# A four-layer attention kernel: the normalisation's reciprocal root as Ln and Exp on ScalarE, and new limits for the planner

## Chip, core and metric

The kernel runs on one core of a Trainium2 chip. The metric is the device time of one execution in microseconds. A core has TensorE (PE, the matrix multiplier, with a separate stream of weight loads), VectorE (DVE), ScalarE (ACT), GpSimd (POOL) and SyncE (SP, which issues DMAs). Each works through its own list of instructions in order and waits on semaphores that the others raise.

## What is computed

One sequence of 2048 tokens with 512 features goes through four layers, A, B, A, B. Each layer adds to its input the result of an attention over the normalised input, with 32 heads of 16 features.

```
x = x + A(layernorm(x));  x = x + B(layernorm(x));  (both once more)

layernorm: (x - mean) / sqrt(var + 1e-5)     # no scale, no shift

A: 4 segments of 512 tokens; per segment and head
   a_dot = softmax(q k^T / 4 + causal mask) v
   a_mem = phi(q) M / (phi(q) z + 1e-6)      # phi(t) = t + 1 if t > 0 else exp(t)
   o = g * a_mem + (1 - g) * a_dot           # g = sigmoid(beta)
   M += phi(k)^T v;  z += sum phi(k)
B: softmax(q k^T / 4) v over all 2048 tokens
both: then o @ wo
```

## The kernel before, in words

The Python program is a planner. It plays the whole work through with estimated durations, and writes five lists of instructions in the order in which its model would start them (`Sched.estimate`, L133; for DVE and POOL `Sched.queue`, L164, and `Sched.resolve`, L180, which models that the two hold each other up at a shared port). The chip gets the lists.

**Units.** The scores are computed transposed, in banks: one PSUM bank holds the scores of 128 keys and 512 queries of one head. A B layer has 32 heads x 4 query segments x 16 key blocks = 2048 such banks. An A layer keeps the causal ten of sixteen 128 x 128 blocks, packed into 2.5 banks for each head and segment: 32 x 4 x 2.5 = 320 banks. Together that is 2 x 2048 + 2 x 320 = 4736. The main loop (`attention`, L2192) goes by units. A unit (`unit`, L1831) takes three banks from the front of the groups that are ready, or two where other banks go to DVE in the same unit: PE writes the scores (K and masked Q, named KB or KA and qm), and **one ACT instruction at L1912 takes the exp of the two or three banks** into pT. PE multiplies pT by V in a later unit; a column of ones in V gives the softmax's denominator.

**Banks on DVE.** DVE takes other banks away from ACT. `dx_first` (L1373) writes at L1381 an integer whose bits, read as bfloat16, are a coarse exp of the score; two further copies with a constant added to the bits are made by POOL (`pool_copy`, L1454, at L1462) or DVE (L1437, and L1480 for two pairs at once). PE multiplies all three by V and adds them up, so that such a bank goes through PE three times and not once. The buffers for it are dxt and, once they are idle, the space of KA, QA, VA, wA and wB; in the profile the groups at L1381 and L1462 carry these names. Which bank may be taken is decided in `dx_pick` (L1301). There TAKEN caps the share of a B group's banks, and TAKEN_A the number of banks of an A group.

**Background.** Projections, normalisation, phi, memory update and output projection are generators (`task_A`, `task_B` and others) that yield what they need and what they cost in PE and DVE time. `background` (L1614) and `bg_one` (L1559) run one step after another between the units, as far as credits allow. A need ("at", n) holds a step back until unit step n, and a need ("free", ...) (in `met`, L1533) until the model has the named buffers ready shortly after ACT's current end; both are used by phi (L962), whose Exp on ACT (L966) is followed two steps later by two DVE instructions (L969, L971).

**Normalisation** (`ln_part`, L856) works on four tiles of 128 tokens at a time, 16 times in all. For each tile DVE computes mean and variance (L864, L866). Then the reciprocal root for the four, on 128 x 4 numbers: at the first normalisation by Sqrt on ACT (L872), a small Exp that brings the table of Exp back (L873), and a reciprocal on DVE (L875). At the other 15 DVE does it alone: add epsilon (L877), a first guess by integer arithmetic on the bits (L879), and two Newton rounds of three instructions (L882, L883, L884), with a yield ahead of each round. `normalize` (L887) applies mean and root to a tile at L893, on DVE, or on POOL where POOL_XN is set; the tile then goes through a transposing DMA (`ln_tiles`, L924). The first normalisation uses `ln_first` (L899) and PE's transposes (L722).

**Limits.** PLAN (from L413) holds 76 rows of limits. `set_limits` (L2187) installs row k when the unit number reaches 20k. The limits say among other things how many banks DVE may take (TAKEN, TAKEN_A), when POOL takes copies or other work (POOL_C, POOL_D, POOL_XN, POOL_PHI, POOL_QM), how late an engine may be for a step to be issued (DVE_LATE, DX_LATE, EARLY, HURRY), and how the background is sorted (ORD).

PE also multiplies by a tile of zeros where its modelled activity falls below a limit (`keep_busy`, L655, and `fill_gap`, L679, issued at L675 and L702). Most matmuls carry line L675 (the helper `mm`), and evacuations of projections L749 (ACT) or L751 (DVE).

Of the kernel before, what the change touches and what calls it, by code (L numbers as in the profile page):

```python
# [5 lines left out]
dt = mybir.dt  # L6
ACT = mybir.ActivationFunctionType
# [11 lines left out]
RSQRT_MAGIC = 1597463007.0  # L19
# [72 lines left out]
class Sched:  # L92
# [86 lines left out]

    def resolve(self):  # L180
# [5 lines left out]
        while i < len(D) or j < len(G):  # L186
            if i < len(D):
                r = D[i]
                x = max(pd + r[2], r[3] + r[1]) - r[1]
            if j < len(G):  # L190
                q = G[j]
                y = max(pg + q[2], q[3] + q[1]) - q[1]
            if j == len(G) or i < len(D) and x <= y:
                if r[4] and j < len(G) and q[4] and y - x < RACE:
                    x = max(x, y + q[1] - PORT)
                if r[4]:
                    for a, z in lg:
                        if a + 20 - RACE < x < z - PORT:
                            x = z - PORT
                    ld.append((x, x + r[1]))  # L200
                pd = r[5] = r[0].end = x + r[1]
                i += 1
            else:
                if q[4]:
                    for a, z in ld:
                        if a < y < z - PORT_G:
                            y = z - PORT_G
                    lg.append((y, y + q[1]))
                pg = q[5] = q[0].end = y + q[1]
                j += 1  # L210
# [199 lines left out]
class Builder:  # L410
# [3 lines left out]
        0: dict(TAKEN_A=1, FILL_DVE=400, MASK_PE=800, PE_LOW=7, GAP=3, QMIN=3, OPART=0, DIV_LATE=2500, PACE=2, DX_LATE=1700, HURRY=1500, POOL_QM=1, POOL_C=0),  # L414
        1: dict(ACT1=300, MARGIN=600, R_LATE=2200, NEAR=5, CR_W=1300, CR_B=1800, R_PAIRS=2, DIV_LATE=800, TAKEN=0.5, DVE_LATE=800, BG_BANK=100, PHI_LATE=300, OPART=3, NEARW=20, POOL_C=2000, DX_LAG=1, POOL_D=2500, REST=8, EARLY=500, POOL_QM=1, DX_FIN=3000, DMA_LATE=1200, TRADE=400, FILL_DVE=400, ORD=-7, PACE=12, DMA_STEPS=2, HOLD_AT=12, PE_B=2),
        2: dict(FILL_DVE=400, MASK_PE=800, GAP=3, BG_BANK=400, QMIN=3, LOW=20, POOL_QM=1, ACT1=600, R_PAIRS=2, PE_LOW=7, DX_LATE=1700, DX_FIN=3000, OPART=0, HOLD_AT=12, PE_A=4, NEAR_A=50, TRADE=0, TAKEN_A=1, PART=3, DMA_LATE=700, CR_B=1200, SLACK=350),
        3: dict(R_LATE=1200, NEARW=40, PAIRS=999, MASK_PE=800, LEVEL=3, TAKEN=0.5, LOW=20, MARGIN=600, TAKEN_A=1, EARLY=300, OPART=0, QUAD=0, FILL=0.47, DX_BANK=900, CR_A=1200, DX_LATE=700, CARRY_W=1500, PART=3, CR_W=2200, HOLD_MAX=0, DVE_LATE=1700, FILL_DVE=400, BUSY_WAIT=500, ACT1=300, QMIN=3, PE_LOW=7, PE_A=6, TRADE=0, DVE_LATE_LOW=2500, POOL_D=2500, PACE=7, PE_B=6, DVE_FIN=1500, ORD=3),
        4: dict(R_LATE=1200, NEARW=40, PAIRS=999, MASK_PE=800, LEVEL=3, TAKEN=0.5, LOW=20, MARGIN=600, TAKEN_A=1, EARLY=300, OPART=0, QUAD=0, FILL=0.47, DX_BANK=900, CR_A=1200, DX_LATE=700, CARRY_W=1500, PART=3, CR_W=2200, HOLD_MAX=0, DVE_LATE=1700, FILL_DVE=400, BUSY_WAIT=500, ACT1=300, QMIN=3, PE_LOW=7, PE_A=6, TRADE=0, DVE_LATE_LOW=2500, POOL_D=2500, PACE=7, PE_B=6),
        5: dict(ACT1=300, NEAR=8, TAKEN_A=1, SLACK=550, PV_SKIP=900, FILL_DVE=400, BACK=8, CR_W=1900, NEARW=40, OPART=0, TAKEN=0.4, LOW=20, DVE_LATE=800, QWAIT=8, HOLD_AT=40, PHI_LATE=0, REST=20, POOL_D=2500, R_LATE=1200, MARGIN=350, EARLY=300, QUAD=0, CR_A=1700, CARRY_W=1500, PART=3, BUSY_WAIT=500, PE_LOW=7, PE_A=6, HURRY=4000, PAIRS=999, LEVEL=3, DX_BANK=900, DX_LATE=700, QMIN=3, TRADE=0, DVE_LATE_LOW=2500, PACE=7, DVE_FIN=1500),
        6: dict(MARGIN=350, R_LATE=1200, DX_LATE=900, TAKEN_A=1, EARLY=300, CARRY_W=1500, PART=3, OPART=2, GAP=3, QUAD=0, QWAIT=8, HOLD_SEGS=2, POOL_XN=1, NEAR=8, SLACK=550, PV_SKIP=900, FILL_DVE=400, CR_W=1900, LOW=20, PHI_LATE=0, REST=12, PE_A=6, POOL_WAIT=0, FIT=3, AHEAD=1000, POOL_QM=1, DVE_LATE=800, POOL_D=2500, LEVEL=1, BACK=8, TAKEN=0.4, BUSY_WAIT=500, QMIN=3, DVE_LATE_LOW=2500, PACE=7, DVE_FIN=200),  # L420
        7: dict(R_LATE=1200, NEARW=40, PAIRS=999, MASK_PE=800, LEVEL=3, TAKEN=0.4, LOW=30, MARGIN=350, TAKEN_A=1, EARLY=300, OPART=3, QUAD=0, FILL=0.47, DX_BANK=900, CR_A=1200, DX_LATE=900, CARRY_W=1500, PART=3, CR_W=2200, HOLD_MAX=0, DVE_LATE=1700, FILL_DVE=400, BUSY_WAIT=500, ACT1=300, DMA_LATE=1200, GAP=3, QWAIT=8, NEAR=8, PE_A=6, POOL_QM=1, DVE_LATE_LOW=2500, PACE=7, DVE_FIN=200, HURRY=1500),
        8: dict(R_LATE=1200, NEARW=40, PAIRS=999, MASK_PE=800, LEVEL=3, TAKEN=0.4, LOW=30, MARGIN=500, TAKEN_A=1, EARLY=300, OPART=3, QUAD=0, FILL=0.47, DX_BANK=900, CR_A=1200, DX_LATE=900, CARRY_W=1500, PART=3, CR_W=2200, HOLD_MAX=0, DVE_LATE=1700, FILL_DVE=400, BUSY_WAIT=500, ACT1=300, DMA_LATE=1200, QWAIT=8, NEAR=8, PV_SKIP=900),
        9: dict(MARGIN=600, NEAR=3, PV_SKIP=100, FILL_DVE=100, BUSY_ROOM=900, FILL=0.4, CR_W=1500, CARRY_W=400, R_PAIRS=2, OPART=2, GAP=3, DVE_LATE=800, QMIN=1, HOLD_AT=40, POOL_QM=1, ACT1=300, DX_LATE=900, REST=8, CR_B=1800, DX_LAG=1, BACK=6, LOW=14, BUSY_WAIT=0, POOL_D=1200, PART=3, PHI_LATE=0, EVAC_ACT=800, RUSH0=40, HURRY=1500, AHEAD=1000),
        10: dict(MARGIN=600, NEAR=3, PV_SKIP=100, FILL_DVE=100, BUSY_ROOM=900, FILL=0.4, CR_W=1500, CARRY_W=400, R_PAIRS=2, OPART=4, GAP=3, DVE_LATE=800, QMIN=1, HOLD_AT=40, POOL_QM=1, ACT1=300, DX_LATE=900, REST=8, CR_B=1800, DX_LAG=1, BACK=6, LOW=14, BUSY_WAIT=500, POOL_D=1200, PART=3, PHI_LATE=0, EVAC_ACT=800, RUSH0=40, HURRY=1500, AHEAD=1000, RUSH=120),
        11: dict(R_LATE=1500, DX_LATE=700, REST=12, NEAR=8, TAKEN_A=1, R_NEAR=50, PV_SKIP=500, FILL_DVE=400, BUSY_ROOM=900, CR_W=1300, DX_LAG=1, LOW=20, HOLD_SEGS=2, BACK=6, R_PAIRS=2, BG_BANK=100, EVAC_ACT=100, EARLY=500, CR_A=1200, POOL_QM=1, POOL_D=1200, DVE_LATE=1700, POOL_C=4000, PORT_FREE=900, PART=0),
# [348 lines left out]
    def setup(self):  # L774
# [16 lines left out]
        def pool(fn, writes, reads=()):  # L791
            self.op("pool", fn, reads=reads, writes=writes)
# [94 lines left out]
    def normalize(self, s, k, i):  # L887
# [7 lines left out]
        if eng == "pool":  # L895
            self.cr_dve += 420
# [1456 lines left out]
```

## Time and profile before

| | us |
|---|---|
| median of three runs | 1659.27 |
| lowest and highest of them | 1659.11, 1660.82 |
| the profiled execution's own time | 1659.6 |
| its span, first to last instruction | 1657.9 |
| the part outside the span | 1.7 |

The granted clock of TensorE in the profiled execution was 0.998 of full speed. The profile's busy time is the time in which an engine has an instruction in work. A group's row gives line, engine, operation, written and read tiles, shape and number; then total busy time and mean ns of one; then the idle time just before, and what ended it. "L1912 <- PE" in a list of waits means that L1912 waited for PE. In a stretch's row a busy time stands for each engine with its number of instructions, then the granted clock, the share of the DMA engines and GB/s.

### The profile page before, as it was taken

The numbers are of one execution on the slowest core, as the hardware profiler recorded it, in microseconds if no ns is written. First come the engines' busy times: TensorE is split into PE (matmuls) and PEld (weight loads), VectorE is DVE, ScalarE is ACT, GpSimd is POOL, SyncE is SP. The second block draws the span as 40 slices with busy tenths as digits, with TensorE's granted clock in tenths as the row PEclk, the third lists the DMA queues.
The fourth block names the chain that finished last, engine by engine and source line by source line (L and its number), as shares of the span: only waits on it lengthen the run. The fifth ranks groups of instructions, "written<-read, shape, count | busy, mean of one in ns | idle before, by whom it ended". The sixth has DMA issues, their size and how long they took to land.

```text
span 1657.9 us, 45400 instructions
## 1 busy us (share of the span) xinstructions
PE 1567.7 (95%) x19612; PEld 565.5 (34%) x19684; DVE 1432.7 (86%) x2387; ACT 1621.5 (98%) x1552; POOL 1206.4 (73%) x1295
## 2 busy tenths in 40 slices
PE   8999999999999999999999998999999999999999
PEld 5553435222223535222235222432222222222236
DVE  5768686989999696999978998878999999999996
ACT  8899999999999999999999999999999999999998
POOL 3332223589899354799775996468999999999985
PEclk9999999999999999999999999999999999999999
DMA  6111211001120232200211101112000200000110
GB/s 185 37 24 26 40 26 29 14 2 30 30 55 14 69 71 43 56 14 11 62 24 40 40 24 39 23 19 53 2 18 20 46 12 16 21 11 11 24 14 19
DMA packets 148425, 54.47 MB, mean 33 GB/s; under 512 B 128768, under 2 KB 147712, under 8 KB 148224
## 3 DMA queue, kind: packets, MB, share of 16 engines
q1 hardware_dynamic: 148224, 51.56, 14.4%
q8 instruction: 154, 2.52, 0.6%
q14 instruction: 47, 0.39, 0.1%
HBM read 18.88 MB, written 2.10 MB: 13 GB/s over the span
## 4 chain that ended last, share of the span: by engine, by line
ACT 58%; PE 24%; DVE 14%; POOL 2%; DMA 1%; issue 1%; SPq 0%; ACTq 0%; DVEq 0%; POOLq 0%
ACT pT L1912 56%; PE ps L675 23%; DVE KA L1381 3%; DVE dxt L1381 2%; DVE wA L1381 2%; ACT amem L966 1%; DVE wB L1381 1%; DMA oT<-ob 1%; POOL dxt L1462 1%; DMA tb<-ub 0%; DVE wA L1480 0%; DVE lnst L864 0%; DVE dxt L1480 0%; DVE oT L1198 0%; DVE VA L1480 0%
## 5 line engine op out<-in xcount | busy, mean ns | idle before, releaser
L1912 ACT ACTIVATE pT<-ps 128x1024 bf16<-128x1024 f32 (+1 forms) x1506 | 1589.5, 1211 | 23.4 <-PE ps L675 20.4
L675 PE MATMUL ps<-qm,KB 32*128 32x512 bf16 x4096 | 543.3, 385 | 54.4 <-ACT pT L1912 35.9
L675 PE MATMUL ps<-pT,VB 128*17 128x512 bf16 x2744 | 475.5, 384 | 3.0 <-DVE wB L1381 1.1
L1462 POOL TENSOR_TENSOR dxt<-dxt,shift 128x512 int32<-128x512 int32 (+1 forms) x300 | 322.7, 1086 | 127.2 <-DVE dxt L1381 92.6
L1381 DVE TENSOR_SCALAR KA<-ps 128x512 uint16<-128x512 f32 (+1 forms) x414 | 322.6, 799 | 20.6 <-PE ps L675 18.4
L675 PEld LDWEIGHTS ps<-qm,KB 32*128 32x128 bf16 x4096 | 140.3, 91 | 556.0 <-ACT pT L1912 443.6
L1381 DVE TENSOR_SCALAR dxt<-ps 128x512 uint16<-128x512 f32 (+1 forms) x346 | 262.5, 774 | 26.2 <-PE ps L675 24.4
L1462 POOL TENSOR_TENSOR QA<-KA,shift 128x512 int32<-128x512 int32 (+1 forms) x192 | 211.2, 1108 | 89.3 <-DVE KA L1381 88.8
L675 PE MATMUL ps<-dxt,VB 128*17 128x512 bf16 x1140 | 243.0, 382 | 0.6 <-POOL dxt L1462 0.6
L675 PEld LDWEIGHTS ps<-pT,VB 128*17 128x17 bf16 x2744 | 110.8, 87 | 274.5 <-issue 256.2
L1462 POOL TENSOR_TENSOR VA<-KA,shift 128x512 int32<-128x512 int32 (+1 forms) x178 | 187.1, 1059 | 14.1 <-DVE QA L1437 6.4
L1926 POOL TENSOR_SCALAR_AFFINE_SELECT pT<-pT 128x256 bf16<-128x256 bf16 (+4 forms) x136 | 70.2, 530 | 174.3 <-ACT pT L1912 174.2
L1462 POOL TENSOR_TENSOR wA<-wA,shift 128x512 int32<-128x512 int32 x150 | 161.8, 1093 | 17.6 <-DVE wA L1381 15.7
L1381 DVE TENSOR_SCALAR wA<-ps 128x512 uint16<-128x512 f32 (+1 forms) x168 | 133.0, 809 | 8.7 <-PE ps L675 7.9
L675 PE MATMUL ps<-wA,VB 128*17 128x512 bf16 x624 | 138.0, 381 | 0.0
L675 PE MATMUL ps<-QA,VB 128*17 128x512 bf16 x474 | 133.5, 381 | 0.0
L1462 POOL TENSOR_TENSOR wB<-wB,shift 128x512 int32<-128x512 int32 (+1 forms) x118 | 126.2, 1083 | 6.9 <-DVE wB L1381 5.2
L675 PE MATMUL ps<-VA,VB 128*17 128x512 bf16 x474 | 130.2, 381 | 0.5 <-POOL VA L1462 0.4
L675 PE MATMUL ps<-KA,VB 128*17 128x512 bf16 x474 | 116.6, 381 | 0.0
L1381 DVE TENSOR_SCALAR wB<-ps 128x512 uint16<-128x512 f32 (+1 forms) x137 | 105.5, 785 | 7.0 <-PE ps L675 6.4
L675 PE MATMUL ps<-wB,VB 128*17 128x512 bf16 x486 | 108.2, 381 | 0.1
L675 PE MATMUL ps<-qm,KA 32*128 32x128 bf16 (+2 forms) x1536 | 93.3, 254 | 10.6 <-ACT pT L1912 7.6
(174 smaller groups left out, 2043.9 us busy)
## 6 DMA issues: line engine op xcount, KB each, us to landing
wB<-in_B_wqkv_dram SPq DMA_DIRECT2D x48, 128.0 KB, 2.4
wA<-in_A_wk_dram SPq DMA_DIRECT2D x16, 128.0 KB, 2.3
wA<-in_A_wq_dram SPq DMA_DIRECT2D x16, 128.0 KB, 2.4
wA<-in_A_wv_dram SPq DMA_DIRECT2D x16, 128.0 KB, 2.4
out_dram<-x SPq DMA_DIRECT2D x8, 256.0 KB, 2.3
x<-in_A_x_dram SPq DMA_DIRECT2D x3, 512.0 KB, 10.9
wB<-in_B_wqkv_dram SPq DMA_DIRECT2D x1, 1536.0 KB, 13.9
oT<-ob SPq DMA_TRANSPOSE x63, 2.5
```

Of the source, the lines that this page charges most:

```text
L675: self.sc.add("pe", lambda e: e.matmul(out, lhsT, rhs, start=start, stop=stop, skip_group_check=True), reads=reads, banks=[(bank, "w", all ...
L966: self.op("act", lambda e: e.activation(et, src, ACT.Exp), reads=bsrc, writes=self.b_amem, ns=1023, gap=915)
L1381: self.op("dve", lambda e: e.tensor_scalar(d, o, SCALE * LOG2E * 128, 127.0 * 128 + EXP_BIAS, op0=ALU.mult, op1=ALU.add), writes=self.b_dx ...
L1462: self.op("pool", lambda e: e.tensor_tensor(d, s, c, ALU.add), reads=src + [self.b_shift] + [first] * k, writes=dst, ns=165 + 1.75 * n, ga ...
L1912: self.sc.add("act", (lambda dst, src: lambda e: e.activation(dst, src, ACT.Exp, scale=SCALE))(dst, src), writes=self.b_pT[slot * 3 + i:sl ...
L1926: self.op("pool", (lambda blk, pat: lambda e: e.affine_select(blk, blk, pattern=pat, compare_op=ALU.is_ge, fill=0.0, base=0, channel_multi ...
```

## The change

The reciprocal root becomes exp(-0.5 ln(var + eps)), in two ACT instructions for all 16 normalisations. One instruction in the setup loads a table set that holds both functions. The Newton rounds on DVE, the Sqrt and the small Exp at the start are gone. At all but the first normalisation the Ln waits for a ("free", ...) need, and the Exp for the next unit step.

```diff
@@ setup
+        self.sc.add("act", lambda e: e.preload_act_table_set("natural_log_exp_and_others"), ns=1283, gap=1283)
         for bk in (SUMS, MISC):
@@ ln_part
         bw = self.b_lnw[k]
-        yield [], 0, 400
-        v, y, tt = w[:, k, 0, :], w[:, k, 1, :], w[:, k, 2, :]
+        v, y = w[:, k, 0, :], w[:, k, 1, :]
         var = st[:, k, :, 7]
-        if (L, s) == (0, 0):
-            self.op("act", lambda e: e.activation(v, var, ACT.Sqrt, bias=self.eps[:, 0:1]), reads=self.b_lnst[k] + [self.b_eps], writes=[bw], ns=230)
-            self.op("act", lambda e: e.activation(self.eps[:, 1:2], self.eps[:, 0:1], ACT.Exp), reads=[self.b_eps], writes=[self.b_eps], ns=1500)
+        first = (L, s) == (0, 0)
+        if not first:
+            yield [("free", [bw], self.b_lnst[k])], 0, 0
+        self.op("act", lambda e: e.activation(v, var, ACT.Ln, bias=self.eps[:, 0:1]), reads=self.b_lnst[k] + [self.b_eps], writes=[bw], ns=300, gap=215)
+        if not first:
+            yield [("at", self.step + 1)], 0, 0
+        self.op("act", lambda e: e.activation(y, v, ACT.Exp, scale=-0.5), reads=[bw], writes=[bw], ns=300, gap=215)
+        if first:
             self.parity()
-            self.op("dve", lambda e: e.reciprocal(y, v), reads=[bw], writes=[bw], ns=165)
-            return k
-        self.op("dve", lambda e: e.tensor_scalar(v, var, LN_EPS, None, op0=ALU.add), reads=self.b_lnst[k], writes=[bw], ns=165)
-        vi, yi = v.bitcast(dt.int32), y.bitcast(dt.int32)
-        self.op("dve", lambda e: e.tensor_scalar(yi, vi, -0.5, RSQRT_MAGIC, op0=ALU.mult, op1=ALU.add), reads=[bw], writes=[bw], ns=165)
-        for it in range(2):
-            yield [], 0, 560
-            self.op("dve", lambda e: e.scalar_tensor_tensor(tt, y, -0.5, y, op0=ALU.mult, op1=ALU.mult), reads=[bw], writes=[bw], ns=165)
-            self.op("dve", lambda e: e.tensor_tensor(tt, tt, v, ALU.mult), reads=[bw], writes=[bw], ns=165)
-            self.op("dve", lambda e: e.scalar_tensor_tensor(y, tt, 1.5, y, op0=ALU.add, op1=ALU.mult), reads=[bw], writes=[bw], ns=165)
         return k
```

Where POOL_XN is set, the normalised tile is made by two POOL instructions with one per-partition operand each, instead of one with two:

```diff
@@ normalize
-        eng = "pool" if self.POOL_XN else "dve"
...
+        if self.POOL_XN:
+            self.op("pool", lambda e: e.tensor_scalar(xn, self.x[:, t, :], mean, 0.0, op0=ALU.subtract, op1=ALU.add), reads=[self.b_x[t], self.b_lnst[k][i]], writes=[self.b_xn[n]], ns=762, gap=720)
+            self.op("pool", lambda e: e.tensor_scalar(xn, xn, rstd, 0.0, op0=ALU.mult, op1=ALU.add), reads=[self.b_lnw[k]], writes=[self.b_xn[n]], ns=762, gap=720)
+        else:
```

In the planner's model of DVE and POOL, an instruction's readiness is worked out again from the moved ends of the DVE and POOL instructions that it waits for:

```diff
+    def late_ready(self, r):
+        op, ready = r[0], r[3]
+        for d in op.deps:
+            if d.eng == "dve" or d.eng == "pool":
+                ready = max(ready, d.end + (SOON.get((d.eng, op.eng)) or LAG[d.eng]))
+        return ready
@@ resolve
-                x = max(pd + r[2], r[3] + r[1]) - r[1]
+                x = max(pd + r[2], self.late_ready(r) + r[1]) - r[1]
...
-                y = max(pg + q[2], q[3] + q[1]) - q[1]
+                y = max(pg + q[2], self.late_ready(q) + q[1]) - q[1]
```

In PLAN, 70 of the 76 rows change, in 1 to 43 limits each; they were chosen by playing the lists through with random delays. The changes that touch who does the work, with the values that hold without an entry in the row (0 for all three):

| limit | rows and values before > after |
|---|---|
| TAKEN_A | 1, 23, 56, 61: 0 > 1; 47: 0 > 2; 15, 69, 70: 0 > 5; 17: 1 > 0 |
| POOL_XN | 8, 24, 28, 48: 0 > 1; 61: 1 > 0 |
| POOL_PHI (1: phi's L969 on POOL) | 6, 20, 21, 26, 35, 42, 46, 73: 0 > 1 |

TAKEN (the share of a B group that DVE may take) rises in 11 rows and falls in 7; POOL_C and POOL_D (how far POOL may be behind DVE to take a copy) rise in 16 and 14 and fall in 10 and 8.

More of the change, by code (lines that the diff above doesn't have):

```diff
@@ L420 @@
-        6: dict(MARGIN=350, R_LATE=1200, DX_LATE=900, TAKEN_A=1, EARLY=300, CARRY_W=1500, PART=3, OPART=2, GAP=3, QUAD=0, QWAIT=8, HOLD_SEGS=2, POOL_XN=1, NEAR=8, SLACK=550, PV_SKIP=900, FILL_DVE=400, CR_W=1900, LOW=20, PHI_LATE=0, REST=12, PE_A=6, POOL_WAIT=0, FIT=3, AHEAD=1000, POOL_QM=1, DVE_LATE=800, POOL_D=2500, LEVEL=1, BACK=8, TAKEN=0.4, BUSY_WAIT=500, QMIN=3, DVE_LATE_LOW=2500, PACE=7, DVE_FIN=200),
+        5: dict(ACT1=300, NEAR=8, TAKEN_A=1, PV_SKIP=900, FILL_DVE=400, BACK=8, CR_W=2200, NEARW=40, OPART=0, TAKEN=0.4, LOW=20, DVE_LATE=800, QWAIT=8, HOLD_AT=40, PHI_LATE=0, REST=20, POOL_D=2500, R_LATE=1200, MARGIN=350, EARLY=300, QUAD=0, CR_A=1700, CARRY_W=1500, PART=3, BUSY_WAIT=500, PE_LOW=7, PE_A=6, HURRY=4000, PAIRS=999, LEVEL=3, DX_BANK=900, DX_LATE=700, QMIN=3, TRADE=0, DVE_LATE_LOW=2500, PACE=7, DVE_FIN=1500, MASK_PE=800, FILL=0.47),
@@ new lines @@
+        23: dict(PAIRS=999, MASK_PE=800, LEVEL=3, TAKEN=0.5, LOW=14, MARGIN=500, TAKEN_A=1, EARLY=300, OPART=0, QUAD=0, FILL=0.4, DX_BANK=900, CR_A=1200, CARRY_W=400, PART=3, CR_W=2200, HOLD_MAX=0, DVE_LATE=1700, FILL_DVE=400, BUSY_WAIT=500, ACT1=300, QMIN=3, PE_LOW=7, TRADE=0, DVE_LATE_LOW=2500, POOL_D=500, ORD=23, BG_BANK=100, EVAC_ACT=1500, PV_SKIP=100, BUSY_ROOM=300, R_PAIRS=2, POOL_QM=1, CR_B=1800, DX_LAG=1, BACK=6, AHEAD=1000, DMA_STEPS=2, PE_B=6, DMA_LATE=0),
+        24: dict(R_LATE=1200, NEARW=40, PAIRS=999, MASK_PE=800, LEVEL=3, TAKEN=0.4, LOW=30, MARGIN=500, TAKEN_A=1, EARLY=300, OPART=3, QUAD=0, FILL=0.47, DX_BANK=900, CR_A=1200, DX_LATE=900, CARRY_W=1500, PART=3, CR_W=2200, HOLD_MAX=0, DVE_LATE=1700, FILL_DVE=400, BUSY_WAIT=500, ACT1=300, DMA_LATE=1200, QWAIT=3, NEAR=8, PV_SKIP=900, SPARE=160, POOL_XN=1),
@@ new lines @@
+        47: dict(ACT1=300, MARGIN=600, R_LATE=2200, EVAC_ACT=800, NEAR=10, CR_W=1300, CR_B=1800, R_PAIRS=2, DIV_LATE=2500, TAKEN=0.5, DVE_LATE=800, BG_BANK=100, PHI_LATE=300, OPART=3, NEARW=20, POOL_C=1000, DX_LAG=1, POOL_D=2500, REST=12, EARLY=500, POOL_QM=1, DX_FIN=3000, DMA_LATE=1200, PE_LOW=7, PORT_FREE=150, TRADE=400, RATE=2, DX_LATE=700, FILL=0.53, CARRY_W=1500, LN1_AT=6, FILL_DVE=400, POOL_WAIT=0, BUSY_ROOM=300, RUSH=40, REST_A=6, TAKEN_A=2, SPARE=60),
+        48: dict(ACT1=200, DX_LATE=700, NEAR=10, PV_SKIP=200, EARLY=500, FILL=0.47, CR_B=1800, CARRY_W=1500, OPART=2, MASK_PE=200, DIV_LATE=800, DVE_LATE=800, BG_BANK=100, QUAD=0, FILL_DVE=400, R_LATE=2200, POOL_C=2000, BACK=8, POOL_D=2500, RUSH0=40, AHEAD=1000, MARGIN=600, PE_B=6, DMA_LATE=700, QMIN=4, DX_FIN=3000, SLACK=250, HURRY=4000, TRADE=0, POOL_QM=1, FIT=3, POOL_XN=1),
@@ L490 @@
+        75: dict(REST=8, SLACK=700, R_NEAR=10, R_PAIRS=2, NEARW=90, PAIRS=999, LEVEL=1, LOW=14, GAP=1, DVE_LATE=800, BG_BANK=400, QUAD=0, POOL_WAIT=300, PV_SKIP=100, BACK=6, FILL=0.47, PART=0, LN1_AT=3, EARLY=300, DIV_LATE=2500, MARGIN=350, POOL_C=1000, ACT1=300, MASK_PE=200, POOL_D=1200, BUSY_ROOM=300, CR_W=1500, TAKEN=0.5, POOL_XN=1, CR_A=1700, CR_LOW=2000, DX_BANK=700, RATE=2, QWAIT=3, DVE_FIN=1500, POOL_QM=1, DMA_LATE=0),
     }
```

140 lines of the change are left out of this document (66 added, 74 removed).

## The prediction

> **What bounds the kernel now.** I read the busy shares and the chain of the page first, then the stretches by stage, then ScalarE's waits, then the groups that the edit touches.
>
> ```profile
> span 1657.9 us, 45400 instructions
> ...
> PE 1567.7 (95%) x19612; PEld 565.5 (34%) x19684; DVE 1432.7 (86%) x2387; ACT 1621.5 (98%) x1552; POOL 1206.4 (73%) x1295
> ...
> ACT 58%; PE 24%; DVE 14%; POOL 2%; DMA 1%; issue 1%; SPq 0%; ACTq 0%; DVEq 0%; POOLq 0%
> ```
>
> ScalarE (ACT) is busy for 98% of the span and holds 58% of the chain; TensorE (PE) holds 24% of it. So a microsecond of ACT work is worth about a microsecond of time, as long as PE follows.
>
> ```profile
> 0.00:300.00 300.00, 278.03 (x4007) 137.98 (x4045) 215.88 (x479) 284.11 (x237) 95.15 (x159) 0.99 0.23 51
> 300.00:550.00 250.00, 237.98 (x2718) 72.62 (x2717) 227.23 (x357) 248.71 (x248) 219.91 (x229) 1.00 0.12 26
> 550.00:700.00 150.00, 142.09 (x1992) 62.50 (x2007) 117.81 (x248) 148.75 (x133) 74.58 (x92) 1.00 0.28 62
> 700.00:850.00 150.00, 145.47 (x1669) 41.88 (x1669) 138.82 (x219) 148.07 (x150) 134.87 (x136) 1.00 0.13 28
> 850.00:900.00 50.00, 46.00 (x758) 24.92 (x761) 39.44 (x68) 48.72 (x44) 28.99 (x37) 1.00 0.14 26
> 900.00:1050.00 150.00, 139.65 (x1554) 41.46 (x1552) 135.50 (x223) 146.93 (x145) 121.00 (x118) 1.00 0.15 37
> 1050.00:1150.00 100.00, 95.28 (x1323) 38.49 (x1325) 82.55 (x149) 98.67 (x92) 63.64 (x77) 1.00 0.18 35
> 1150.00:1600.00 450.00, 429.98 (x4532) 113.10 (x4528) 431.94 (x577) 446.75 (x459) 435.06 (x420) 1.00 0.08 18
> ```
>
> The columns after the stretch are PE, weight load, DVE, ACT and POOL in us. After the start, ACT is near its limit in every stage. VectorE (DVE) is not: 72% in 0 to 300, 79% in 550 to 700 and in 850 to 900, 83% in 1050 to 1150, but 90 to 96% in the other four. Freed DVE time is therefore worth something in those four only. In the weak stages DVE is idle for 84.1 + 32.2 + 10.6 + 17.5 = 144 us: there something other than its time keeps units from it.
>
> ```profile
> ACT pT L1912 <- PE ps L675: 20.4, 48, 1.3
> ```
>
> Before its main exp (L1912) ACT waits for PE 48 times, 20.4 us in all; that is nearly all the idle time that a better order could give back.
>
> **The normalisation, on ACT.** Fifteen of the sixteen normalisations each get two new ACT instructions, a Ln with a pointer bias and an Exp. The first one already has Sqrt and an Exp.
>
> ```profile
> 6.26 0.30 ACT L872 ACTIVATE lnw<-lnst,eps 128x4 f32<-128x4 f32 x1 [1.67 <-DVE par L827]
> 6.58 1.28 ACT L873 ACT_TABLE_LOAD   x1
> 7.87 0.20 ACT L873 ACTIVATE eps<-eps 128x1 f32<-128x1 f32 x1
> ```
>
> ```profile
> 15.74 0.22 ACT L841 ACTIVATE gtok<-bet 128x32 f32<-128x32 bf16 x1
> 15.86 0.22 ACT L841 ACTIVATE gout<-bet 128x32 f32<-128x32 bf16 x1
> ```
>
> The Sqrt on the same tile with the same bias takes 0.30 us (L872; columns: start, us). Two small Exps one behind the other take 0.22 us each, yet start 0.12 us apart, so 0.10 us overlaps. Thirty instructions cost at least 30 x 0.12 = 3.6 us, and without any overlap 15 x (0.30 + 0.22) = 7.8 us. I take the overlap off both, since the rows show ACT running such instructions back to back: 15 x (0.20 + 0.12) = **+4.8 us**. The Trainium skill (ScalarE: Activation LUTs, "Rules for kernel authors") budgets about 0.3 us for each ACTIVATE beside its elements, which is 9.1 us by estimate and would make the forecast below 1654; the 0.12 us between two starts speaks against it.
>
> **The normalisation, on DVE.** Gone are the groups of the magic-number guess and of the two Newton rounds:
>
> ```profile
> L882 DVE SCALAR_TENSOR_TENSOR lnw<-lnw 128x4 f32<-128x4 f32 x30 | 6.3, 209 | 0.7
> L883 DVE TENSOR_TENSOR lnw<-lnw 128x4 f32<-128x4 f32 x30 | 5.7, 191 | 1.0
> ...
> L884 DVE SCALAR_TENSOR_TENSOR lnw<-lnw 128x4 f32<-128x4 f32 x30 | 4.9, 162 | 1.0
> L877 DVE TENSOR_SCALAR lnw<-lnst 128x4 f32<-128x4 f32 x15 | 4.0, 269 | 0.4
> ...
> L879 DVE TENSOR_SCALAR lnw<-lnw 128x4 int32<-128x4 int32 x15 | 3.1, 206 | 0.5
> ```
>
> That is 6.3 + 5.7 + 4.9 + 4.0 + 3.1 = 24.0 us, 1.6 us for each normalisation. What it buys depends on where they lie. L877 runs once in each of the fifteen; in the loaded stages it stands five times:
>
> ```profile
> 300.00:550.00 250.00, 1.10 (x2) 1.00 0.12 26
> 700.00:850.00 150.00, 0.17 (x1) 1.00 0.13 28
> 900.00:1050.00 150.00, 0.49 (x2) 1.00 0.15 37
> ```
>
> The other ten lie where DVE has idle time anyway, and I count nothing for them. Five give 8.0 us. What DVE can do with it is to take more banks of scores from ACT. A bank's prices come from these rows:
>
> ```profile
> L1912 ACT ACTIVATE pT<-ps 128x1024 bf16<-128x1024 f32 x1065 | 1015.2, 1092 | 10.0 <-PE ps L675 8.0
> L1912 ACT ACTIVATE pT<-ps 128x1536 bf16<-128x1536 f32 x441 | 628.0, 1496 | 13.5 <-PE ps L675 12.4
> ```
>
> ```profile
> sum 1658.00, DVE 810.20; mean DVE 810.20
> ```
>
> ```profile
> sum 1658.00, DVE 120.29; mean DVE 120.29
> ```
>
> ```profile
> sum 1658.00, DVE 73.32; mean DVE 73.32
> ```
>
> ACT's two-bank exp costs 1015.2 / 1065 = 0.953 us and its three-bank exp 628.0 / 441 = 1.424 us: a bank taken away saves 0.471 us. The scores have 4736 banks (2048 for each B layer, 320 for each A layer), and ACT does 2 x 1065 + 3 x 441 = 3453, so DVE takes 1283. DVE spends on them 810.20 us in the first pass (L1381, the first sum) and 120.29 + 73.32 us in the shifted copies that are left to it (L1437, L1480): 0.78 us a bank. So 8.0 us are 10 banks, **-4.8 us** of ACT; bounds are nothing, and all 24.0 us, which are 31 banks and 14.5 us. The new root thus pays for itself and no more.
>
> **The table loads at the start.**
>
> ```profile
> 6.81 0.73 DVE L906 TENSOR_SCALAR xn<-x,lnst,lnw 128x512 bf16<-128x512 bf16 x2
> ```
>
> Three loads become one. From the Sqrt's start to DVE's first normalised tile there is 0.55 us; Ln and Exp with 0.30 + 0.22 us and a hop are as long. The load at 6.58 lies beside DVE's normalising and PE's transposes. I count nothing; with that cover gone it would be a gain of up to 1.3 us.
>
> **The limits.** Of 76 rows, each valid for 20 units, 70 differ. Row k starts near the 20k-th L1912. Most limits have no price in the trace. One kind has: TAKEN_A, the banks of a causal (A) group that DVE may take, rises from 0 to 1 in rows 1 and 23 and from 0 to 2 in row 47 (the other rises, in rows 15, 56, 61, 69 and 70, stand where few or no A groups are left). Twenty units hold some 60 banks, or six A groups, so at most 6 + 6 + 12 = 24 banks; other groups lie between them, and I take half: 12 banks x 0.471 = **-5.7 us**, from nothing to -11.3. These rows lie at about 30, 560 and 1080 us, in stages with DVE idle, so DVE has the 9.4 us. Moving normalised tiles (POOL_XN, rows 8, 24, 28, 48) and phi to POOL frees DVE in the same weak stages; I count nothing, and it is hidden by POOL's own idle time there (75.4 of 150 us in 550 to 700). Of the 20.4 us of PE waits I let the new order win a fifth, **-4 us**. That is a choice: nothing in the trace fixes it, and the bounds are 20.4 us saved and as much again lost. The corrected readiness in the planner has no instruction of its own; its effect is in that term.
>
> **Sum:** 1659.6 (span 1657.9 and 1.7 around it) + 4.8 - 4.8 - 5.7 - 4 = 1649.9. The median of the runs is 0.3 lower than the profiled execution, so the forecast is **1650 us**.
>
> **The rivals.** *PE takes over.* A bank on DVE goes through PE three times, not once:
>
> ```profile
> L675 PE MATMUL ps<-dxt,VB 128*17 128x512 bf16 x1140 | 243.0, 382 | 0.6 <-POOL dxt L1462 0.6
> ...
> L675 PE MATMUL ps<-woB,zero 128*32 128x512 bf16 (+1 forms) x183 | 59.5, 380 | 0.6 <-DVE QA L751 0.3 <-DVE KA L1381 0.2
> ```
>
> Two more passes of 243.0 / 1140 = 0.213 us are 0.43 us of PE, nearly the 0.471 us that ACT saves. Against it: 59.5 us of PE's busy time in the second group multiply by zeros as padding and can shrink. For it: PE holds 24% of the chain. Then neither 4.8 nor 5.7 us is won, and 1659.3 + 4.8 - 4 gives 1660.
>
> *DVE waits for the Exp.* This one ends slower. The normalised tile on DVE now needs an Exp that stands in ACT's queue behind main exps, and only one step lies between. Behind that tile on DVE stand first passes and evacuations, for which PE waits, and ACT for PE. The price is up to one three-bank exp each, 15 x 1.42 = 21.3 us. With the 4.8 us of banks lost to it, 1659.3 + 4.8 - 5.7 - 4 + 21.3 = 1676; if half passes through, 1665. From a passed-on wait of (5.7 + 4 - 4.8) / 15 = 0.33 us the kernel is slower. Phi has the same pair of engines, 24 times, with two steps between:
>
> ```profile
>   ACT amem L966: 0.5, 1
> ```
>
> ```profile
> ACT amem L966 <- DVE phq L971: 0.7, 1, 0.7
> ```
>
> DVE waited there 0.5 us for ACT in all, and ACT 0.7 us for DVE. That speaks against it, though one step is half the room.
>
> *The tables are switched.* Every function so far got its own load (L820, L872, L873). Should the program switch at each Ln and back, 30 loads of 1.28 us make 38.5 us on ACT, and 1650 becomes 1688. One explicit load ahead of all speaks against it. The Trainium skill (ScalarE: Activation LUTs, "What ACT_TABLE_LOAD costs") adds a drain of 1380 ns to each switch; by it the 30 would cost 80 us and the time 1730. The trace doesn't show that drain: the load at 6.58 follows an instruction that ended at 6.56, and its successor starts at 7.87. The same page ("Table sets: the hidden batching unit") names one set with both functions, which this trace cannot show.
>
> **How the numbers follow.** Forecast 0.63, PE takes over 0.15, DVE waits 0.17, tables 0.05. The bounds of the likeliest are 1633 (12 banks, and all 20.4 us of waits) and 1656. A measurement of this kernel can tell about 0.2%, 3.3 us, from no change. The forecast's cases lie beyond that: faster 0.63. PE's case lies nearly all within: same 0.14. The rest is slower: 0.23. The range, 1633 to 1666, takes in the forecast, PE's case and half-passed waits; some 0.18 is left out, most of it above.
>
> **What would show it.** Right: one table load in the trace; 30 more small ACT instructions at 0.1 to 0.3 us each; L882 to L884 gone and DVE some 10 us busier elsewhere; 15 to 30 fewer banks on L1912; ACT's waits for PE below 20 us. Wrong: banks on ACT unchanged at 3453 with PE's share of the chain up (PE took over); idle time of DVE ahead of xn, released by ACT's lnw (DVE waits); loads at every normalisation. A gain far beyond 20 us would mean that the limits, which I could price least, moved many more banks than the A groups' twelve.

## The result, and the profile after

| | before | changed |
|---|---|---|
| median, us | 1659.28 | 1668.13 |
| lowest to highest of six runs, us | 1658.85 to 1660.82 | 1666.33 to 1670.19 |
| profiled execution, us | 1659.6 | 1669.98 |

The ratio is 1.0054 (95% interval 1.0041 to 1.0067): the change makes the kernel 0.5% slower. The forecast was 1650 and faster.

First the changed kernel's page, its busy shares and its chain:

```profile
span 1668.0 us, 45578 instructions
...
PE 1581.1 (95%) x19797; PEld 571.1 (34%) x19797; DVE 1406.3 (84%) x2219; ACT 1623.1 (97%) x1572; POOL 1260.2 (76%) x1315
...
ACT 63%; PE 25%; DVE 6%; POOL 3%; DMA 2%; issue 1%; ACTq 0%; POOLq 0%; DVEq 0%
```

The span grew by 10.1 us, ACT's busy time by only 1.6 (1621.5 to 1623.1). ACT stood idle 8.5 us longer. DVE was busy 26 us less, mostly because its root (24.0 us) is gone, and POOL 54 us more. Next ACT's groups in the changed kernel (columns: busy us, mean ns, then the idle time ahead and what ended it):

```profile
L1915 ACT ACTIVATE pT<-ps 128x1024 bf16<-128x1024 f32 x1047 | 1004.6, 1103 | 11.2 <-PE ps L682 9.3
L1915 ACT ACTIVATE pT<-ps 128x1536 bf16<-128x1536 f32 x455 | 652.4, 1502 | 14.6 <-PE ps L682 13.7
...
L881 ACT ACTIVATE lnw<-lnst,eps 128x4 f32<-128x4 f32 x16 | 5.5, 341 | 3.4 <-DVE par L835 3.1 <-DVE lnst L874 0.3
L884 ACT ACTIVATE lnw<-lnw 128x4 f32<-128x4 f32 x16 | 3.8, 236 | 0.0
L824 ACT ACT_TABLE_LOAD x1 | 1.3, 1283 | 0.8 <-PEq L2341 0.8
```

One table load is left, and Ln and Exp cost what was expected of them. But ACT does 2 x 1047 + 3 x 455 = 3459 banks, six more than before: although all that DVE time is free, no bank moved from ACT to DVE.

Where was the time lost? Busy times by stretch show it; the row below adds up 550 to 750 us, before and then changed:

```profile
sum 200.00, PE 190.90 PEld 76.56 DVE 164.81 ACT 198.05 POOL 121.91; mean PE 95.45 PEld 38.28 DVE 82.41 ACT 99.03 POOL 60.95
```

```profile
sum 200.00, PE 185.56 PEld 75.01 DVE 147.26 ACT 189.46 POOL 129.62; mean PE 92.78 PEld 37.50 DVE 73.63 ACT 94.73 POOL 64.81
```

ACT lost 8.6 us in these 200 us alone, as much as in the whole span. PE and DVE did less too; only POOL did more. The timeline of POOL there, in the changed kernel, shows what it did (start and duration in us):

```profile
638.58 3.63 POOL L972 TENSOR_SCALAR phk<-phk 128x1024 bf16<-128x1024 bf16 x1
...
642.24 3.63 POOL L972 TENSOR_SCALAR phq<-QA 128x1024 bf16<-128x1024 bf16 x1
...
647.82 3.62 POOL L972 TENSOR_SCALAR phq<-QA 128x1024 bf16<-128x1024 bf16 x1
```

and DVE and ACT beside it:

```profile
642.25 1.58 DVE L974 TENSOR_TENSOR phk<-phk,amem 128x1024 bf16<-128x1024 bf16 x1 [4.21 <-POOL phk L972]
```

```profile
643.86 1.06 ACT L969 ACTIVATE amem<-QA 128x1024 bf16<-128x1024 bf16 x1 [2.68 <-DVE phk L974]
```

PE waited too, for the evacuation (VB, L758) that stands behind this instruction in DVE's list:

```profile
PE ps L682 <- DVE VB L758: 3.5, 1, 3.5
```

That is a whole chain of waits: phi's first step, now on POOL, takes 3.63 us where the planner booked 1.2. DVE stands 4.21 us for it at the head of its list, PE 3.5 us for the evacuation behind it, and ACT 2.68 us for DVE.

The second place is at 699 to 717 us, where POOL makes four normalised tiles. A copy for a bank (wA, L1465) stands behind two of them; PE waits for the copy, and ACT's main exp for PE:

```profile
702.28 2.00 POOL L895 TENSOR_SCALAR xn<-x,lnst 128x512 bf16<-128x512 bf16 x1
704.38 0.69 POOL L896 TENSOR_SCALAR xn<-xn,lnw 128x512 bf16<-128x512 bf16 x1
705.03 1.04 POOL L1465 TENSOR_TENSOR wA<-wA,shift 128x512 int32<-128x512 int32 x1
```

```profile
PE ps L682 <- POOL wA L1465: 2.7, 2, 2.5
```

```profile
706.88 1.02 ACT L1915 ACTIVATE pT<-ps 128x1024 bf16<-128x1024 f32 x1 [2.52 <-PE ps L682]
```

The groups of the two new kinds of POOL work:

```profile
L895 POOL TENSOR_SCALAR xn<-x,lnst 128x512 bf16<-128x512 bf16 x12 | 24.8, 2064 | 0.0
L972 POOL TENSOR_SCALAR phq<-QA 128x1024 bf16<-128x1024 bf16 x3 | 10.9, 3625 | 0.0
L896 POOL TENSOR_SCALAR xn<-xn,lnw 128x512 bf16<-128x512 bf16 x12 | 8.3, 695 | 1.5 <-ACT lnw L884 0.5
...
L972 POOL TENSOR_SCALAR phk<-phk 128x1024 bf16<-128x1024 bf16 x1 | 3.6, 3631 | 0.0
```

The subtraction of the mean (L895) takes 2.06 us, booked at 0.72. The multiplication by the root (L896), on a tile of the same size, takes 0.70, as booked. The unbooked time is 24.8 - 12 x 0.72 + 10.9 + 3.6 - 4 x 1.2 = 25.9 us. **Theory POOL:** this surprise is the loss. **Rivals:** the order is worse as such, since DVE waits for the Exp or the new limits are no better; or ACT's thirty instructions are the loss.

### The profile page after: what moved, and what is told of

Its sections match the earlier page's. It is cut to its first block, busy times and chain, and to the rows that moved or that the text cites. A ratio compares the mean times of both kernels' runs of the same rounds, so it can differ in the third digit from the quotient of the medians.

```text
span 1668.0 us, 45578 instructions
## 1 busy us (share of the span) xinstructions
PE 1581.1 (95%) x19797; PEld 571.1 (34%) x19797; DVE 1406.3 (84%) x2219; ACT 1623.1 (97%) x1572; POOL 1260.2 (76%) x1315
## 3 DMA queue, kind: packets, MB, share of 16 engines
q1 hardware_dynamic: 148224, 51.56, 14.2%
## 4 chain that ended last, share of the span: by engine, by line
ACT 63%; PE 25%; DVE 6%; POOL 3%; DMA 2%; issue 1%; ACTq 0%; POOLq 0%; DVEq 0%
ACT pT L1915 62%; PE ps L682 25%; ACT amem L969 1%; DMA phq<-amem 1%; DVE KA L1384 1%; DVE dxt L1384 1%; POOL xn L895 1%; DVE wA L1384 1%; POOL wA L1465 1%; POOL dxt L1465 1%; DMA tb<-ub 1%; DVE wB L1384 0%; DVE lnst L872 0%; POOL VA L1465 0%; POOL xn L896 0%
## 5 line engine op out<-in xcount | busy, mean ns | idle before, releaser
L1465 POOL TENSOR_TENSOR dxt<-dxt,shift 128x512 int32<-128x512 int32 (+1 forms) x293 | 319.2, 1099 | 117.4 <-DVE dxt L1384 83.5
L1384 DVE TENSOR_SCALAR KA<-ps 128x512 uint16<-128x512 f32 (+1 forms) x398 | 312.1, 801 | 29.5 <-PE ps L682 27.0
L1384 DVE TENSOR_SCALAR dxt<-ps 128x512 uint16<-128x512 f32 (+1 forms) x331 | 257.7, 793 | 25.0 <-PE ps L682 22.8
L682 PE MATMUL ps<-dxt,VB 128*17 128x512 bf16 x1128 | 249.2, 381 | 0.1
L1465 POOL TENSOR_TENSOR QA<-KA,shift 128x512 int32<-128x512 int32 x179 | 196.6, 1108 | 56.0 <-DVE KA L1384 55.9
L1465 POOL TENSOR_TENSOR VA<-KA,shift 128x512 int32<-128x512 int32 x176 | 190.9, 1094 | 15.0 <-DVE QA L1440 9.5
L1929 POOL TENSOR_SCALAR_AFFINE_SELECT pT<-pT 128x256 bf16<-128x256 bf16 (+4 forms) x123 | 64.7, 539 | 165.2 <-ACT pT L1915 165.0
L1465 POOL TENSOR_TENSOR wA<-wA,shift 128x512 int32<-128x512 int32 (+1 forms) x160 | 169.7, 1074 | 17.5 <-DVE wA L1384 14.5
L1465 POOL TENSOR_TENSOR wB<-wB,shift 128x512 int32<-128x512 int32 (+1 forms) x133 | 142.6, 1087 | 10.0 <-DVE wB L1384 8.3
L1384 DVE TENSOR_SCALAR wB<-ps 128x512 uint16<-128x512 f32 (+1 forms) x139 | 112.7, 827 | 8.9 <-PE ps L682 8.2
L682 PE MATMUL ps<-VA,pT 128*128 128x51 bf16 (+1 forms) x2488 | 102.6, 188 | 0.9 <-DVE ob L2033 0.4
```

The source lines that it names most:

```text
L682: self.sc.add("pe", lambda e: e.matmul(out, lhsT, rhs, start=start, stop=stop, skip_group_check=True), reads=reads, banks=[(bank, "w", all ...
L1384: self.op("dve", lambda e: e.tensor_scalar(d, o, SCALE * LOG2E * 128, 127.0 * 128 + EXP_BIAS, op0=ALU.mult, op1=ALU.add), writes=self.b_dx ...
L1465: self.op("pool", lambda e: e.tensor_tensor(d, s, c, ALU.add), reads=src + [self.b_shift] + [first] * k, writes=dst, ns=165 + 1.75 * n, ga ...
L1929: self.op("pool", (lambda blk, pat: lambda e: e.affine_select(blk, blk, pattern=pat, compare_op=ALU.is_ge, fill=0.0, base=0, channel_multi ...
```

## The experiments

The kernels e1, e2, e3 and e5 keep the changed kernel's five lists, instruction for instruction, so that little but durations differs; e4 adds instructions to ACT's list alone. Each ratio is to the kernel before, measured anew beside the run; its median lay between 1658.8 and 1660.8 us. Different experiments are therefore best compared by their ratios.

**e1, both POOL instructions made cheap**

```diff
-  tensor_scalar(xn, x, mean, 0.0, op0=ALU.subtract, op1=ALU.add)      # L895
+  tensor_scalar(xn, x, mean, 0.0, op0=ALU.mult, op1=ALU.add)
-  tensor_scalar(dst, src, 0.0, 1.0, op0=ALU.max, op1=ALU.add)         # L972, where on POOL
+  tensor_scalar(dst, src, 1.0, 1.0, op0=ALU.mult, op1=ALU.add)
```

> The changed kernel's lists, instruction for instruction, but POOL's subtraction of the mean (L895) becomes a multiplication and POOL's maximum in phi (L972) too, so that both should take what the planner booked for them (about 0.7 and 1.2 us, in place of 2.0 and 3.6). The normalised tiles of three normalisations and four of phi's pieces are computed wrongly. Theory POOL: the unbooked 12 x 1.3 + 4 x 2.4 = 25 us of POOL hold up copies, phi and with them PE and ACT between 600 and 720 us: the time falls from 1668 to 1659 to 1662, and the half-clock windows near 642 and 707 us go. Theory order (DVE waits for the Exp on ACT, or the new limits are worse as such): it stays at 1666 to 1669.

Measured: 1655.72 us, ratio to the kernel before 0.9969 (0.9957 to 0.9981), faster than even theory POOL expected. L895 now takes 0.78 us in the mean and L972 1.2 and 1.05 (phq, phk). The sum of 550 to 750 us in e1:

```profile
sum 200.00, PE 190.88 PEld 76.67 DVE 154.26 ACT 198.03 POOL 122.75; mean PE 95.44 PEld 38.33 DVE 77.13 ACT 99.02 POOL 61.37
```

ACT's 198.03 is that of the kernel before. Theory POOL holds: sixteen instructions with unexpected durations cost 1668.1 - 1655.7 = 12.4 us; by the ratios, 1.0054 - 0.9969 of 1660 us, it is 14.1. Behind them lay a gain.

**e2 and e3, one of them at a time**

> As the kernel with both, but only POOL's subtraction of the mean is replaced (twelve instructions, normalised tiles of three normalisations computed wrongly). Theory POOL: 12 x 1.3 = 16 us of POOL less, of which the waits around 700 us (one of 2.5 us on ACT) go: 1664 to 1666. Theory order: 1666 to 1669.

> As the kernel with both, but only POOL's maximum in phi is replaced (four instructions; four of phi's pieces come out wrong). Theory POOL: 4 x 2.4 = 10 us of POOL less, three of them in a row at 638 to 651 us, where ACT waited 2.7 us and PE fell to half clock for 6.8 us: 1663 to 1665. Theory order: 1666 to 1669.

Measured: 1661.60 (ratio 0.9999, 0.9990 to 1.0008) and 1663.51 (1.0015, 1.0006 to 1.0024), against 1668.13 for the changed kernel: 6.5 us from the subtraction, 4.6 from the maximum (9.1 and 6.5 by the ratios). They add up to about the whole. The subtraction cost more than was expected for e2.

**e4, ACT's new instructions twice**

```diff
         self.op("act", ... ACT.Exp, scale=-0.5), ...)
+        for z in range(2 if not first else 0):
+            self.op("act", ... the same Exp, into an unread place ..., ns=0, gap=0)
```

> The changed kernel's lists with two more small Exps on ACT behind each of the 15 normalisations' Exps, which the planner doesn't book (their results go to places that nobody reads). Thirty more small ACT instructions are as many as the change added. My prediction's price of 0.16 us each says +4.8 us: 1673. If the time falls on waits and not on ACT's own work, less than +2: 1668 to 1670.

Measured: 1670.03 (1.0053, 1.0041 to 1.0065; the changed kernel has 1.0054). ACT is busy 1625.7 us, 2.6 more. The difference in time can't be told from nothing, so thirty small ACT instructions don't explain a loss of 9 us. Nobody waits for the added ones, so that this tells of ACT's time alone; what the wait for the root's Exp costs is the matter of e12.

**e5, which operations are slow on POOL**

```diff
-  op0=ALU.subtract, op1=ALU.add                                   # L895
+  subtract-add, add-add, subtract-mult, mult-add, mult-subtract, max-add in turn
-  op0=ALU.max, op1=ALU.add                                        # L972, where on POOL
+  max-add, add-max, add-mult, mult-add in turn
```

> The changed kernel's lists; each of POOL's twelve normalising instructions (L895) gets one of six pairs of operations, each pair twice: subtract-add, add-add, subtract-mult, mult-add, mult-subtract, max-add, always with the mean as the first operand; phi's four on POOL (L972) get max-add, add-max, add-mult, mult-add. Values of these tiles are wrong. Which pairs are slow tells why the two instructions cost 2.0 and 3.6 us: if a pair is fast only with a multiplication first and an addition second, mult-add alone takes 0.7 us (1.2 for phi) and the others 2.0 (3.6); if the subtraction (or the maximum) itself is slow, add-add is fast too.

One run, with a time near the changed kernel's (1667.99). Its POOL timeline at the first tiles of the second normalisation done there, which are the third to sixth pair in turn:

```profile
599.88 2.27 POOL L897 TENSOR_SCALAR xn<-x,lnst 128x512 bf16<-128x512 bf16 x1
...
602.90 0.69 POOL L897 TENSOR_SCALAR xn<-x,lnst 128x512 bf16<-128x512 bf16 x1
...
605.77 2.24 POOL L897 TENSOR_SCALAR xn<-x,lnst 128x512 bf16<-128x512 bf16 x1
...
608.82 2.00 POOL L897 TENSOR_SCALAR xn<-x,lnst 128x512 bf16<-128x512 bf16 x1
```

Subtract-mult, mult-subtract and max-add are slow; mult-add alone is fast, and so it is at its second turn. Add-add took 2.00 us both times, so it isn't the subtraction. Of phi's pairs, the second to fourth in turn stand here in order of time:

```profile
637.93 3.64 POOL L976 TENSOR_SCALAR phk<-phk 128x1024 bf16<-128x1024 bf16 x1
...
641.59 1.05 POOL L976 TENSOR_SCALAR phq<-QA 128x1024 bf16<-128x1024 bf16 x1
...
644.39 1.52 POOL L976 TENSOR_SCALAR phq<-QA 128x1024 bf16<-128x1024 bf16 x1
```

They are add-max, add-mult and mult-add; max-add, the first, ran at 189.7 us in 3.62. The last row ran beside a DVE instruction (644.32 to 645.00 us); in e1, mult-add took 1.04 to 1.05 three times, and 1.52 once, beside the same instruction. So a multiplication and an addition together are fast, in either order here, and every other pair tried is slow.

**e6, e7 and e8, planned anew**

```diff
# e6: PLAN without the POOL_XN and POOL_PHI that the change set
# e7: the durations that the trace showed
-  ns=762, gap=720   (L895)          +  ns=2040, gap=2000
-  ns=1250, gap=1200 (L972 on POOL)  +  ns=3670, gap=3630
# e8: the kernel before, with the changed ln_part and the table load only
```

> The changed kernel, planned anew with POOL_XN and POOL_PHI set in none of the rows that the change gave them (DVE does those 12 tiles and 4 pieces). Theory POOL: what the unbooked POOL time cost comes back, though DVE has some 7 us more to do and every list differs: 1656 to 1661. Rival (the new limits are worse as such, or DVE waits for the Exp): 1665 or more.

> The changed kernel, planned anew with the durations that the trace showed: 2.04 us booked for POOL's subtraction and 3.67 us for its maximum, same limits. The work stays on POOL, and the planner now sees it coming. If it is the surprise that costs, 1657 to 1662; if it is the occupied POOL, 1663 to 1668.

> The kernel before with the new root alone (Ln and Exp on ACT, one table load), its old limits and old readiness rule, planned anew. My prediction put this part at nothing (4.8 us more on ACT, 4.8 us less through DVE): 1657 to 1663. If DVE's wait for the Exp passes on to ACT, 1665 or more.

Measured: 1700.44 (1.0258, 1.0241 to 1.0274), 1740.20 (1.0496, 1.0482 to 1.0510) and 1705.07 (1.0280, 1.0266 to 1.0294). No theory said so much. The three have one thing in common: the planner wrote new lists from limits chosen for others.

**e11, planned anew for nothing**

```diff
-  bn_aggr ... ns=180        +  bn_aggr ... ns=190        # the kernel before
```

> The kernel before with one booked duration changed by 10 ns (the aggregation of the variance, 190 in place of 180), no instruction or limit changed; the planner then writes other lists. If limits hold only for the very lists that they were chosen on: 1690 to 1710, like the three kernels planned anew. If those three were slow for what was changed in them: 1657 to 1664.

Measured: 1722.14 (1.0375, 1.0361 to 1.0389). Ten booked nanoseconds cost 62 us. In e11 ACT's main exps look like this:

```profile
L1912 ACT ACTIVATE pT<-ps 128x1024 bf16<-128x1024 f32 x1018 | 976.8, 1083 | 13.5 <-PE ps L675 9.9
L1912 ACT ACTIVATE pT<-ps 128x1536 bf16<-128x1536 f32 x492 | 700.4, 1497 | 37.0 <-PE ps L675 34.7
```

They are 2 x 1018 + 3 x 492 = 3512 banks, 59 more than before, and twice the waiting. The limits hold only for the lists on which they were chosen, and e6 to e8 tell nothing of the parts that they changed.

**e9, the same lists, whole computation, fast operations**

```diff
-  tensor_scalar(xn, x, mean, 0.0, op0=subtract, op1=add)             # L895
+  tensor_scalar(neg, mean, -1.0, 0.0, op0=mult, op1=add)             # POOL, 128x1, not booked
+  tensor_scalar(xn, x, 1.0, neg, op0=mult, op1=add)
   # phi, where its first step is on POOL: max(t + 1, min(exp t, 1))
-  POOL max(t, 0) + 1;  DVE tensor_tensor min with exp t
+  POOL t * 1 + 1;      DVE scalar_tensor_tensor (exp t min 1) max it
```

> The changed kernel's lists with the whole computation, in the pairs of operations that were fast on POOL: the tile is multiplied by 1 and the negated mean added (mult-add; a small POOL instruction that the planner doesn't book negates the mean, twelve times), and phi is max(t + 1, min(exp t, 1)), so that POOL has mult-add and DVE a scalar_tensor_tensor in place of its minimum, four times. Theory POOL: 0.7 and 1.0 us in place of 2.0 and 3.6 bring nearly all back that the kernel with both replaced won: 1655 to 1659, below the kernel before. Theory order: 1666 to 1669.

Measured: 1656.66, ratio 0.9981 (0.9972 to 0.9990). This version beats both kernels. It computes all that the changed kernel computes, so that e1's gain doesn't hang on what e1 leaves out.

**e10 and e13, the new root in the old lists**

```diff
+  # after planning the kernel before: take out the eight DVE instructions of each root;
+  # put Ln and Exp into ACT's list at the first place that ends
+  at = next(i for i, o in enumerate(acts) if o.end > r["aggr"].end + 60)      # e13: + 1300
```

> The kernel before with its lists kept, only that after planning the eight DVE instructions of each root (and the first one's reciprocal) are taken out, and Ln and Exp are put into ACT's list where the variance is ready, with the one table load. This is the root's own worth, without any other limit or order. My prediction: 4.8 us more on ACT, and what DVE wins can move no bank in a fixed list, so +2 to +5: 1661 to 1664. If small ACT instructions hide in ACT's waits: 1658 to 1660.

Measured: 1675.40 (1.0086, 1.0072 to 1.0100), far over both. ACT's Ln waited at the head of its list:

```profile
L2327 ACT ACTIVATE lnw<-lnst,eps 128x4 f32<-128x4 f32 x15 | 4.5, 301 | 6.6 <-DVE lnst L866 5.9 <-DVE QB L751 0.5 <-DVE KA L751 0.2
```

So it was put too early, with 5.9 us of waits for the variance; e13 puts it later.

> As the new root in the old lists (e10), but Ln and Exp stand 1.3 us later in ACT's list, so that ACT should not wait for the variance. If e10's 15 us came from those waits and what followed from them, this one is within 5 us of the kernel before, by the 5.0 us that ACT's busy time grew: 1660 to 1665. If the root itself is dear (DVE running early against its plan, or waiting for the Exp): 1670 or more.

Measured: 1664.78 (1.0026, 1.0015 to 1.0037), that is 4.3 us more than the kernel before (2.5 to 6.1). In e13 the same group waits no more:

```profile
L2327 ACT ACTIVATE lnw<-lnst,eps 128x4 f32<-128x4 f32 x15 | 4.9, 328 | 0.0
```

**e12, no wait for the Exp**

```diff
# e1, with DVE's tile
-  tensor_scalar(xn, x, mean, rstd, ...)
+  tensor_scalar(xn, x, mean, eps, ...)        # and no wait for ACT
```

> The kernel with both POOL instructions replaced, same lists, and DVE's normalising instruction takes a constant in place of the root, so that it doesn't wait for the Exp on ACT (the layers' values are wrong). DVE waited 5.7 us for it in 7 places. Theory DVE waits: half or more passes on, 1650 to 1653 against 1655.7. Theory POOL as the whole cause: 1655 to 1657.

Measured: 1656.31 (0.9974, 0.9965 to 0.9983); e1 has 0.9969. The changed kernel's group, with 5.7 us of waits, and that of e12:

```profile
L898 DVE TENSOR_SCALAR xn<-x,lnst,lnw 128x512 bf16<-128x512 bf16 x48 | 27.7, 597 | 7.4 <-ACT lnw L884 5.7 <-DMA xT<-xn 1.7
```

```profile
L898 DVE TENSOR_SCALAR xn<-x,lnst,eps 128x512 bf16<-128x512 bf16 x48 | 27.1, 583 | 1.7 <-DMA xT<-xn 1.7
```

The waits are gone and the time is the same within the intervals: they cost nothing that shows.

## Why the prediction was wrong, point by point

- **The failed step** is one sentence of the part on limits: that moving tiles and phi to POOL counts nothing, "hidden by POOL's own idle time there". It gave the two instructions no duration of its own, and so took over the planner's 0.7 and 1.2 us. They cost 2.06 and 3.63 us. And POOL's idle time over a whole stage was no cover. The tiles at 699 to 717 us lie at the border of the weak stage, and there POOL had hardly any idle time in the kernel before (17.77 of 18.00 us busy, the last of the row's five busy times):

```profile
699.00:717.00 18.00, 17.89 (x207) 4.91 (x207) 17.43 (x26) 18.00 (x20) 17.77 (x19) 1.00 0.08 18
```

  Phi's three at 638 to 651 us did find POOL with idle time, but they stood close together, and DVE, PE and ACT waited behind them in turn. Price: 12 to 14 us (e1), more than the 8.9 us that the kernel lost. The trace of before held a row that looks like the new instructions and would have confirmed the wrong price:

```profile
L1789 POOL TENSOR_SCALAR qm<-QB,par 128x512 bf16<-128x512 bf16 x102 | 75.5, 752 | 0.0
```

  It has the engine, the instruction, the size and the booked 0.72 us of L895, but its operations are a multiplication and an addition. The code gave the better hint: the kernel before booked 2.18 us for a subtraction followed by a multiplication on POOL.
- **ACT's two instructions, +4.8:** the time fits. With the old lists the new root costs 4.3 us (e13, 2.5 to 6.1). That isn't the two instructions alone: in e13's profiled run ACT's busy time grew by 3.6 us although two table loads of 1.28 us were gone, which makes about 6 us for the instructions, and ACT waited 2.4 us for a DMA ahead of phi's Exps, which it didn't before.
- **Five normalisations' DVE time buys ten banks, -4.8:** wrong. DVE did 1277 banks in the changed kernel, 1283 before. A fixed list can't use freed time, and the new one didn't either: DVE's busy time fell by 26.4 us.
- **TAKEN_A, 12 banks, -5.7:** wrong as a count of banks, by the same 3459. Without the POOL surprise the changed lists are 5.0 us faster than the kernel before (e1). If the new root costs them the 4.3 us that it costs the old lists (e13), the new order and limits won 9.3 us. That this is about the 9.7 that I gave to limits is luck, as it didn't come through fewer banks. ACT's waits for PE ahead of the main exps in e1 are 14.2 us, against 20.4 before: the fifth (4 us) that I let the order win was 6.2 us. The row of e1 in the waits of ACT (us in total, times, longest us):

```profile
ACT pT L1915 <- PE ps L682: 14.2, 41, 1.1
```

  ACT also makes four evacuations of projections fewer (nine at L749 before, five at L756 now), 2.4 us in all. That these are the other 3 us wasn't tried.
- **Table loads:** one is left, and counting nothing for the other two was right: ACT's first copy of the transposed tiles (xT) starts at 8.15 us, against 8.04 before.
- **Rival "PE takes over":** PE's share of the chain went from 24 to 25% only. No.
- **Rival "DVE waits for the Exp":** it ended on the right side for the wrong reason. The waits are there, seven times, 5.7 us, and pass on nothing (e12). What I had from it is the mechanism's form, a long instruction at the head of a list, on the wrong engine.
- **The range** ended at 1666, 2 us short. The DVE rival reached 1676; a price for POOL's unseen instructions was missing.

## What to carry to other kernels

An instruction that the trace doesn't contain has no known duration, whatever the planner books for it: look for the nearest row with the same pair of operations on the same engine (the same instruction and size aren't enough), and where there is none, bound it widely. Idle time of an engine hides added work only if it lies where the work lies, so read it there and not over a whole stage; three long instructions in a row stall everyone who waits for that list, and so do two in a list that is full. Compare parts of such a change in fixed lists: where limits are fitted to one plan, a plan written anew for nothing can cost more than the change itself (62 us here).

## What the runs showed of the hardware

- POOL's tensor_scalar on 128x512 bf16 takes 0.69 us in the median with mult-add and 2.00 to 2.27 us with subtract-add, add-add, subtract-mult, mult-subtract or max-add (the mean being a per-partition operand); on 128x1024 with constants 1.04 to 1.05 us with mult-add or add-mult (1.52 beside a DVE instruction) and 3.6 us with max-add or add-max. From the two sizes the slow pairs cost (3.63 - 2.00) / 512 = 3.2 ns an element, the fast (1.045 - 0.692) / 512 = 0.69 ns; that is an estimate, as the two sizes differ in their operands too. Why the pair matters stays open. The Trainium skill (GPSIMD Engine Reference, "4.1 Engine selection") calls one-input elementwise work on GpSimd roughly line-rate. The fast pairs come near that, with 0.69 us against 0.41 on DVE (L893 before); the slow ones, at 2.00, don't.
- After the lulls TensorE ran at half its clock. Two stretches of the changed kernel (the last columns are clock, DMA share and GB/s):

```profile
643.00:646.00 3.00, 1.52 (x14) 0.76 (x15) 2.04 (x5) 2.14 (x2) 3.00 (x4) 0.50 0.00 0
646.00:649.00 3.00, 3.00 (x24) 1.18 (x22) 1.07 (x2) 2.65 (x3) 3.00 (x5) 0.50 0.21 44
```

  Four matmuls of the projection (wB, xT, 128x512) took 1.02 us at 638.56 us, ahead of the lull, and 1.88 at 646.70. So a stall can cost twice there, once while PE has no work and once while it catches up. The clock was 0.50 again at 708 to 710 us. In e1 the granted clock was 1.000 over the span, in the changed kernel's profiled run 0.994. How much of the 12 to 14 us is the slow clock wasn't separated. Of the changed kernel's six runs the one with 0.998, the clock of the kernel before, took 1666.33 us, still 7 us more than that kernel, which speaks for the waits as the larger part.
